# Second layer of batches 4 to 7 of a Nyström attention and MLP kernel: eight half-size block products replaced by seven

## The chip, the cores and the metric

The kernel runs on one core of one Trainium2 chip. The metric is the device time of one execution in microseconds, the median of several runs.

## The reference

The reference is an attention of the Nyström kind followed by an MLP with a residual. q, k and v are 8 batches x 8 heads x 576 tokens x 64. The attention's output, with heads side by side, is x: 8 batches x 576 tokens x 512 columns.

```python
xn = (x - mu) / np.sqrt(var + 1e-06) * g_ln
ch = np.maximum(xn @ w_ch1, 0.0) @ w_ch2
return (x + ch)
```

w_ch1 is 512 x 2048 (the first layer) and w_ch2 is 2048 x 512 (the second layer). The document is about the product with w_ch2.

## The kernel before, in words

The matmul operands are fp16, and sums are fp32 in PSUM. Tokens lie in 36 blocks of 128 rows; two batches are nine blocks. An even batch has four blocks in its second layer and leaves its last 64 tokens to the next batch; an odd batch has five.

For each batch the work is attention (`attention2`, for batches 1, 2, (3, 4), (5, 6), 7 together as grouped), rows of x (`rows_of`), statistics of x (`measure`, `deviations`), first layer (`first_layer`) and second layer (`second_layer`). The first layer writes the hidden values, after the ReLU, transposed into `hT`: 128 partitions x 16 chunks of the hidden dimension x tokens, fp16. One `hT` tile exists for even and one for odd batches. ScalarE or VectorE empties the first layer's PSUM tiles (`chunk`), whichever is estimated to be free first.

`second_layer(b)` takes block after block. For each it holds one of four PSUM banks, adds up 16 matmuls (one per chunk of the hidden dimension, hT as the stationary operand of 128x128, `w2_16` as the moving one of 512 columns), and then `finish_block` lets VectorE multiply by the token's 1/deviation and add x, into `xblk`. `store` writes the block out by two DMAs on SyncE's queue (SP). The very last block is done in two halves of 256 columns.

W2 comes in through the ring of six staging buffers ("stg") that also takes q, k and v. Its tiles of 4608 bytes per partition are free again when their cast to fp16 is done.

**What sets the order.** All instructions of all engines keep the order in which the program emits them. While it builds the program, the class `Clock` (line 72) keeps an estimate of when each engine is free and each tile written; `took` (line 108) holds an engine's cost per operation and `note` (line 122) books an instruction. `run` (line 1340) has four generators (attentions, first layers, rows of batch 0, second layers), each of which yields the estimated time at which its next step could start. It takes the first of them, in this order, that could start now. So the second layer is the filling where nothing else can go. Between two steps `help_out` (line 1268) hands out side work: stores, loads, casts on GpSimd, and on VectorE transposes, sums and statistics, wherever the estimate says that the engine is about to be free. `first_layer(b)` may start once `second_layer(b - 1)` has begun. Attention holds one of the four banks while it iterates (`mine`), and the first layer's `product_of_heads` (line 1103) needs two free banks.

`keep_tail` (line 1185) is a GpSimd copy at the begin of an even batch's second layer, which puts its last 64 tokens into the next batch's `hT`.

Of the kernel before, what the change touches and what calls it, by code (L numbers as in the profile page):

```python
# [20 lines left out]
def kernel(  # L21
# [40 lines left out]
    def name_of(x):  # L62
        return x.tensor.name if hasattr(x, "tensor") else x.name

    parted = {}

    def key_of(ap):

        n = name_of(ap)
        return f"{n}:{ap.offset // parted[n]}" if n in parted else n  # L70

    class Clock:


        WAY = 55.0

        def __init__(self):
            self.free = dict.fromkeys(("PE", "DVE", "Activation", "Pool", "SP"), 0.0)
# [13 lines left out]

        def calm(self, n):

            return self.fetched if self.count + n >= self.mark else 0.0

        def at(self, *tiles):
            return max([self.wrote.get(name_of(t), (0.0, ""))[0] for t in tiles] + [0.0]) + self.WAY

        def at_key(self, ap):  # L100
            return self.wrote.get(key_of(ap), (0.0, ""))[0] + self.WAY

        def idle(self, *tiles):

# [3 lines left out]
        def took(self, i, e, n, m):  # L108
            op = type(i).__name__
            if e == "Activation":  # L110
                return 190 + 0.79 * n
            if e == "Pool":
                return 100 + 0.92 * n if "Copy" in op else 280 + 1.76 * n
            if "Stats" in op:
                return 690 if m > 100 else 180
            if n == 1024:
                return 900
            if "Transpose" in op:
                return 110 + 1.15 * n
            return 140 + 1.15 * max(n, m if "Reduce" in op else 0)  # L120

        def note(self, i):
            e = str(i.engine).rsplit(".", 1)[-1]
            outs = [a.bass_ap for a in i.outs if hasattr(a, "bass_ap")]
            ins = [a.bass_ap for a in i.ins if hasattr(a, "bass_ap")]
            size = [[k for _, k in a.ap] for a in outs + ins]
            count = []
            for dims in size:
                n = 1
                for k in dims[1:]:  # L130
                    n *= k
                count.append(n)
            ready = 0.0
            for a in ins:
                t, who = self.wrote.get(key_of(a), (0.0, e))
                if who != e:
                    ready = max(ready, t + self.WAY)
            for a in outs:
                for t, who in (self.wrote.get(key_of(a), (0.0, e)), self.used.get(key_of(a), (0.0, e)),
                               (self.begun.get(key_of(a), 0.0), "")):  # L140
                    if who != e:
                        ready = max(ready, t + self.WAY)
            if type(i).__name__ == "InstDMACopy":
                start = max(self.free[e], ready)
                self.free[e] = start + (580 if e == "SP" else 100)
                self.wire = max(start + 1650, self.wire) + count[0] * size[0][0] * 4 / 370.0
                done = self.wire + 600
                start = done
            elif e == "PE":
                cols = count[0]  # L150
                self.count += 1
                if self.count >= self.mark:
                    self.mark += self.BLOCK
                    ready = max(ready, self.fetched)
                    self.fetched = max(self.now(), ready) + self.FETCH
                rows_, cols_ = tuple(i.tile_size)
                self.cells.append((self.now(), cols / 2.4 * rows_ * cols_ / 128 ** 2))
                if tuple(i.tile_size) == (128, 128):
                    if self.small:
                        self.free[e] = max(list(self.lanes.values()) + [self.free[e]]) + 100  # L160
                        self.small, self.lanes = False, {}
                    start = max(self.free[e], ready)
                    self.free[e] = start + max(cols / 2.4 + 3, 56)
                    done = self.free[e] + 160
                else:
                    if not self.small:
                        self.small, self.lanes = True, {}
                        self.free[e] += 100
                    lane = tuple(i.tile_position)
                    start = max(self.free[e], ready, self.lanes.get(lane, 0.0))  # L170
                    self.lanes[lane] = start + max(cols / 2.4, 70)
                    self.free[e] = start + 6
                    done = self.lanes[lane] + 160
            else:
                start = max(self.free[e], ready)
                done = self.free[e] = start + self.took(i, e, count[0], max(count[1:] + [0]))
            for a in ins:
                n = key_of(a)
                self.used[n] = max(self.used.get(n, (0.0, e)), (done, e))
            for a in outs:  # L180
                n = key_of(a)
                self.wrote[n] = max(self.wrote.get(n, (0.0, e)), (done, e))

    clock = Clock()

# [1029 lines left out]
    def blocks_0_and_1():  # L1215
# [10 lines left out]
        for u in range(2):  # L1226
            finish_block(0, u, accs[u][0])
            banks.release(accs[u][1])

    def second_layer(b):  # L1230
        hT = hTs[b]
        if b == 0:
            yield from blocks_0_and_1()
        blocks = range(4 + b % 2) if b else (2, 3)
        for u in blocks:
# [32 lines left out]
    def help_out(hurry=False):  # L1268

        while True:  # L1270
            now = clock.now() + 100
            begun = len(unstored)
            while unstored and (hurry or clock.at(unstored[0][1]) <= now):
                store(*unstored.pop(0))
            for c in sets:
                if c.loads:
                    if (stage.next("stg") <= now and clock.free["SP"] <= now + 500
                            and clock.wire <= now + AHEAD):
                        c.next_load()
                        begun = -1  # L1280
                    break
            for c in sets:
                if c.casts:
                    if clock.free["Pool"] <= now + 600 and c.cast_ready() <= now + 600:
                        c.next_cast()
                        begun = -1
                    break
            if clock.free["DVE"] <= now + lead():
# [23 lines left out]
    current, begun_first = [0], [0]  # L1312

    def attentions():
        for c in sets:
# [5 lines left out]
    def first_layers():  # L1321
        for b in range(B):
            yield lambda: 0.0 if b == 0 or (b in ready and current[0] == b - 1
                                            and (b <= LAST_WHOLE or len(centered) == 4)) else NEVER
            yield from first_layer(b)
            first_done.add(b)
            if b == 0:
                keep_tail(0)

# [108 lines left out]
```

## Time and profile before

| | us |
|---|---|
| median of three runs (290.29 to 291.4) | 291.2 |
| the profiled execution | 291.77 |
| its span, first to last instruction | 290.0 |
| TensorE matmuls busy | 274.0 (94%) |
| VectorE busy | 187.1 (65%) |
| ScalarE busy | 160.1 (55%) |
| GpSimd busy | 141.7 (49%) |

The mean granted clock of TensorE is 0.987 of full speed. A matmul of 128x512 in the second layer lasts 385 ns on average in the records, since neighbours overlap; the pace of a stream of them is read from what waits for them. The profile names engines PE (TensorE), PEld (its weight loads), DVE (VectorE), ACT (ScalarE), POOL (GpSimd) and SP (SyncE). Most lines of the code are reached through two helpers, so nearly all matmuls carry line 240 and nearly all other instructions line 234; the names of the tiles tell them apart. In a window's row the columns are length, busy us and count for PE, PEld, DVE, ACT and POOL, then granted clock, the DMA engines' share and GB/s. In a timeline row they are start, length, engine, line, operation, shapes, count, and in brackets the engine's idle time before and what ended it.

The last load of q, k and v ends near 150 us. From then on only stores use the queue.

### The profile page before, as it was taken

The numbers are of one execution on the slowest core, as the hardware profiler recorded it, in microseconds if no ns is written. First come the engines' busy times: TensorE is split into PE (matmuls) and PEld (weight loads), VectorE is DVE, ScalarE is ACT, GpSimd is POOL, SyncE is SP. The second block draws the span as 40 slices with busy tenths as digits, with TensorE's granted clock in tenths as the row PEclk, the third lists the DMA queues.
The fourth block names the chain that finished last, engine by engine and source line by source line (L and its number), as shares of the span: only waits on it lengthen the run. The fifth ranks groups of instructions, "written<-read, shape, count | busy, mean of one in ns | idle before, by whom it ended". The sixth has DMA issues, their size and how long they took to land.

```text
span 290.0 us, 8202 instructions
## 1 busy us (share of the span) xinstructions
PE 274.0 (94%) x3426; PEld 147.9 (51%) x3426; DVE 187.1 (65%) x412; ACT 160.1 (55%) x282; POOL 141.7 (49%) x171
## 2 busy tenths in 40 slices
PE   7888996998899999999889999999999999999994
PEld 7644553345444565444445645556445644564443
DVE  3558975699999875997888284878265373422222
ACT  2567955128851787448889755567277732570000
POOL 4378779899998999999980008400003001000000
PEclk9999999599999999999999999999999999999999
DMA  7999999979545499873800112111120113112333
GB/s 244 381 390 386 387 388 390 299 243 329 168 161 150 133 307 335 240 242 108 287 8 3 36 31 48 39 38 36 41 64 12 37 36 75 37 38 61 80 76 75
DMA packets 23374, 46.68 MB, mean 161 GB/s; under 512 B 2212, under 2 KB 2472, under 8 KB 23336
## 3 DMA queue, kind: packets, MB, share of 16 engines
q1 hardware_dynamic: 23176, 46.02, 49.5%
q8 instruction: 27, 0.44, 0.6%
q10 hardware_dynamic: 160, 0.13, 0.2%
q14 instruction: 11, 0.09, 0.1%
HBM read 36.70 MB, written 9.44 MB: 159 GB/s over the span
## 4 chain that ended last, share of the span: by engine, by line
PE 53%; DVE 14%; POOL 13%; DMA 12%; issue 4%; ACT 1%; SPq 1%; POOLq 0%; DVEq 0%; ACTq 0%
PE bank L240 38%; PE psh L240 12%; DMA stg<-in_v_dram 5%; DMA wstg<-in_moe_w_ch_dram 5%; POOL nat L234 4%; POOL asum L234 3%; POOL natv L234 3%; DVE m L234 2%; DVE six L234 2%; DVE w L234 2%; DMA stg<-in_k_dram 2%; DVE part L234 2%; DVE xblk L234 1%; DVE xT L234 1%; POOL w L234 1%
## 5 line engine op out<-in xcount | busy, mean ns | idle before, releaser
L240 PE MATMUL bank<-w,hT 128*128 128x512 f16 (+1 forms) x592 | 148.5, 379 | 0.5 <-issue 0.5
L240 PEld LDWEIGHTS <-hT 128*128 128x128 f16 x592 | 54.8, 98 | 53.6 <-issue 9.9
L234 ACT ACTIVATE hT<-psh 128x576 f16<-128x576 f32 x111 | 69.0, 651 | 22.3 <-PE psh L240 21.6
L240 PE MATMUL psh<-ea,m 128*128 128x288 f16 x512 | 76.5, 286 | 3.1 <-ACT hT L234 1.8
L240 PEld LDWEIGHTS <-m 128*128 128x128 f16 x512 | 48.6, 98 | 27.6 <-issue 9.4
L234 DVE SCALAR_TENSOR_TENSOR xblk<-bank,rstd,xblk 128x512 f32<-128x512 f32 (+1 forms) x37 | 26.8, 728 | 34.8 <-PE bank L240 34.8
L234 POOL CAST natv<-stg 64x1152 f16<-64x1152 f32 (+1 forms) x23 | 26.7, 1161 | 31.4 <-PE pscv L240 22.4
L234 POOL CAST nat<-stg 128x1152 f16<-128x1152 f32 x28 | 32.5, 1180 | 2.0 <-DMA stg<-in_k_dram 1.1
L234 POOL TENSOR_TENSOR ea<-ea,lns 128x576 f16<-128x576 f16 x14 | 17.8, 1286 | 31.6 <-ACT lns L234 31.6
L234 ACT COPY xblk<-bank 128x512 f32<-128x512 f32 (+1 forms) x34 | 19.0, 595 | 18.5 <-PE bank L240 18.4
L234 DVE BATCH_NORM_STATS2 six<-xblk 128x6 f32<-128x512 f32 x36 | 24.3, 676 | 2.6 <-ACT xblk L234 2.5
L234 DVE STREAM_TRANSPOSE xT<-nat 128x576 uint32<-128x576 uint32 x28 | 21.5, 766 | 2.5 <-POOL nat L234 2.5
L234 ACT CAST m<-bank 128x512 f16<-128x512 f32 x30 | 17.0, 588 | 7.0 <-PE bank L240 7.0
L234 DVE CAST m<-bank 128x512 f16<-128x512 f32 x18 | 12.4, 687 | 12.9 <-PE bank L240 12.8
L234 DVE TENSOR_REDUCE part<-xT 128x32 f16<-128x576 f16 x28 | 20.4, 746 | 0.3
L234 ACT ACTIVATE lns<-psd 128x576 f32<-128x576 f32 x16 | 10.3, 646 | 18.1 <-PE psd L240 15.1
L234 POOL TENSOR_TENSOR asum<-asum 128x256 f32<-128x256 f32 (+1 forms) x28 | 17.2, 615 | 2.2
L234 POOL COPY hT<-hT 128x1024 f16<-128x1024 f16 x4 | 4.2, 1038 | 28.9 <-PE bank L240 28.9
L234 POOL TENSOR_TENSOR asum<-nat 128x512 f32<-128x512 f16 x14 | 16.8, 1202 | 1.1
L234 DVE SCALAR_TENSOR_TENSOR st<-st,bank 128x128 f16<-128x128 f16 (+2 forms) x36 | 11.1, 308 | 7.3 <-PE bank L240 7.3
L240 PE MATMUL bank<-zcbd,ea 128*128 128x256 f16 (+1 forms) x80 | 14.5, 275 | 1.2 <-DVE m L234 0.8
L234 DVE TENSOR_SCALAR hT<-psh 128x576 f16<-128x576 f32 x17 | 12.8, 753 | 4.1 <-PE psh L240 3.6
(114 smaller groups left out, 277.6 us busy)
## 6 DMA issues: line engine op xcount, KB each, us to landing
stg<-in_q_dram SPq DMA_DIRECT2D x16, 576.0 KB, 5.5
stg<-in_k_dram SPq DMA_DIRECT2D x16, 576.0 KB, 5.2
stg<-in_v_dram SPq DMA_DIRECT2D x16, 576.0 KB, 6.2
out_dram<-xblk SPq DMA_DIRECT2D x70, 128.0 KB, 2.3
wstg<-in_moe_w_ch_dram SPq DMA_DIRECT2D x16, 512.0 KB, 7.0
out_dram<-xblk ACTq DMA_DIRECT2D x2, 64.0 KB, 2.1
out_dram<-xblk SPq DMA_DIRECT2D x2, 64.0 KB, 2.2
g_rows<-in_moe_g_ln_dram SPq DMA_DIRECT2D x1, 2.0 KB
```

Source lines behind the costliest of these rows:

```text
L234: return lambda *args, **kw: keep(getattr(self.engine, op)(*args, **kw))
L240: keep(nc.tensor.matmul(o, l, r, start=start, stop=stop, tile_position=(rb, cb), skip_group_check=(skip or cb != 0)))
```

## The change

For batches 4 to 7 the four blocks of 128 tokens that the second layer has in common are computed as one product of 512 tokens x 2048 x 512 columns, cut in halves along all three dimensions. Instead of eight products of halves there are seven (256 tokens x 1024 x 256 columns each, 16 matmuls of 256 columns), of mixed operands. The fifth block of batches 5 and 7 stays as it was.

- *Mixes of W2*, once: four tiles t1 to t4 of 128 x 8 x 256 fp16 by GpSimd, each in four subtractions of 512 elements per partition (`mix_w2`). They use four of the six staging buffers, after the last load; two more buffers become s1 and s2, the scratch tiles for mixes of hT.
- *Mixes of hT*, per batch: s1 = h21 + h22, s2 = s1 - h11, h21 = h11 - h21 in place (`mix_ahead`, once the batch's first layer is emitted and s1 and s2 are free), and h12 = h12 - s2 in place within the products. Each is two VectorE instructions of 1024 elements per partition.
- *Products*, per batch, in the order P1 to P7: h11 w11 into bank a; h12 w21 into bank e; s2 t2 on top of a; s1 t1 into bank c; h21 t3 on top of a; h12 w22 on top of c; h22 t4 on top of a. After a product VectorE adds its bank to a quarter of x, two instructions of 128x256, 14 per batch in place of four of 128x512. A product on top of a bank can begin when the bank has been added. s1 and s2 are set free for the next batch after P4.
- *The builder's estimates*: other costs per operation for GpSimd and VectorE, an overlap of neighbouring instructions on one engine, another transfer rate and a delay that grows with the queue, other costs of small matmuls, and dependencies tracked by parts of a tile. They add no instruction but decide about the order of all of them.

Cut to its core:

```diff
 class Clock:
+        OVERLAP = {"Activation": 110, "DVE": 80, "Pool": 30}
...
-            return self.fetched if self.count + n >= self.mark else 0.0
+            return self.fetched if self.count + n + (20 if late() else 0) >= self.mark else 0.0
...
             if e == "Pool":
+                if n == 1024 and name_of(i.outs[0].bass_ap) in mixed_:
+                    return 2080
+                if "Ptr" in op:
+                    return 100 + 1.29 * n
                 return 100 + 0.92 * n if "Copy" in op else 280 + 1.76 * n
+            if n == 1152 and "Copy" in op:
+                return 760
...
+            if n >= 512 and (n == 576 or op == 'InstTensorCopy'):
+                return 100 + 1.13 * n
             if n == 1024:
-                return 900
+                return 690 if name_of(i.outs[0].bass_ap) in mixed_ else 900
...
-                self.wire = max(start + 1650, self.wire) + count[0] * size[0][0] * 4 / 370.0
-                done = self.wire + 600
+                self.wire = max(start + 1650, self.wire) + count[0] * size[0][0] * 4 / 385.0
+                done = self.wire + 600 + min(2200, 0.6 * (self.wire - start - 1650))
...
-                    self.lanes[lane] = start + max(cols / 2.4, 70)
-                    self.free[e] = start + 6
+                    self.lanes.update((x, start + max(cols / 2.4, 30)) for x in lane)
+                    self.free[e] = start + (8 if rows_ == 64 and cols < 128 else 4)
...
-                done = self.free[e] = start + self.took(i, e, count[0], max(count[1:] + [0]))
+                done = start + self.took(i, e, count[0], max(count[1:] + [0]))
+                self.free[e] = done - self.OVERLAP[e]
...
+    def mix_w2():
...
+            if n <= 4:
+                x, y = ((w12, w11), (w22, w2_mix[0]), (w22, w12), (w21, w2_mix[min(1, n - 1)]))[n - 1]
+                for k in range(0, HK, 2):
+                    w2_left.append((t[:, k:k + 2, :], x[:, k:k + 2, :], y[:, k:k + 2, :]))
+        if w2_left:
+            o, x, y = w2_left.pop(0)
+            pool.tensor_tensor(out=o, in0=x, in1=y, op=ALU.subtract)
+
+    def mix(o, left, right, op, k):
+        n = ds(k, 4)
+        dve.tensor_tensor(out=o[:, n, :], in0=left[:, n, :], in1=right[:, n, :], op=op)
...
+    def seven_products(b):
+
+        while b not in h_mixed:
+            yield lambda: NEVER if b not in h_mixed and len(w2_mix) < 6 else 0.0
+            if b not in h_mixed:
+                if hTs[b].name not in mixed_:
+                    yield lambda: clock.at_key(hTs[b][:, MCH - 1, 0:P])
+                mix_ahead()
...
+        def product(to, left, right, first=True):
+            bank, t = to
+            for i in range(2):
+                for k in range(HK):
+                    yield ((lambda: 0.0) if i or k % 4 else
+                           lambda: max(clock.at_key(left[:, k, 0:P]), clock.at_key(right[:, k, :]),
+                                       0.0 if k else clock.idle(banks.tiles[bank])))
+                    MM(t[:, i, :], left[:, k, ts(i, P)], right[:, k, :],
+                       start=first and k == 0 and i == 0, stop=k == HK - 1, skip=True)
+
+        def add(half, col, to, done=False):
+            for i in range(2):
...
+                dve.scalar_tensor_tensor(out=o, in0=to[1][:, i, :], scalar=rstds[b][:, u:u + 1],
+                                         in1=o, op0=ALU.mult, op1=ALU.add)
...
+        yield banks.next
+        a = bank()
+        yield from product(a, h11, w11)
+        early = b in rstds
+        if early:
+            add(0, 0, a)
+        yield banks.next
+        e = bank()
+        yield from product(e, h12, w21)
+        yield from finished(b)
+        if not early:
+            add(0, 0, a)
+        yield from product(a, s2, t2, False)
+        add(0, 0, e)
+        banks.release(e[0])
+        yield banks.next
+        c = bank()
+        add(0, 1, a)
+        for k in (0, 4):
+            mix(h12, h12, s2, ALU.subtract, k)
+        yield from product(c, s1, t1)
+        in_use.clear()
+        add(1, 1, c)
+        yield from product(a, h21, t3, False)
+        add(1, 1, a)
+        yield from product(c, h12, w22, False)
+        add(0, 1, c, True)
+        banks.release(c[0])
+        yield from product(a, h22, t4, False)
+        add(1, 0, a, True)
+        banks.release(a[0])
+
     def second_layer(b):
...
         blocks = range(4 + b % 2) if b else (2, 3)
+        if b >= FAST:
+            yield from seven_products(b)
+            blocks = blocks[4:]
```

`FAST` is 4. In `help_out`, after the casts and before VectorE's other side work, `mix_w2` is called where no load is left and GpSimd is about to be free, and `mix_ahead` where the six tiles exist and VectorE is about to be free.

More of the change, by code (lines that the diff above doesn't have):

```diff
@@ L63, in name_of, with keys_of @@
         return x.tensor.name if hasattr(x, "tensor") else x.name
-    parted = {}
+    parted, mixed_ = {}, set()
     def key_of(ap):
+        return keys_of(ap)[0]
+    def keys_of(ap):
         n = name_of(ap)
-        return f"{n}:{ap.offset // parted[n]}" if n in parted else n
+        if n not in parted:
+            return [n]
+        at = [ap.offset]
+        for step, k in list(ap.ap)[1:]:
+            if step >= parted[n]:
+                at = [o + step * i for o in at for i in range(k)]
+        if n in mixed_:
+            return [f"{n}:{o // parted[n]}:{int(o % parted[n] >= 256)}" for o in at]
+        return [f"{n}:{o // parted[n]}" for o in at]
     class Clock:
         WAY = 55.0
+        OVERLAP = {"Activation": 110, "DVE": 80, "Pool": 30}
         def __init__(self):
@@ L101, in at_key, with idle_key @@
             return self.wrote.get(key_of(ap), (0.0, ""))[0] + self.WAY
+        def idle_key(self, ap):
+            n = key_of(ap)
+            return max(self.wrote.get(n, (0.0, ''))[0], self.used.get(n, (0.0, ''))[0]) + self.WAY
         def idle(self, *tiles):
@@ L132, in note @@
                 count.append(n)
+            reads = [n for a in ins for n in keys_of(a)]
+            writes = [n for a in outs for n in keys_of(a)]
             ready = 0.0
[L134 to L140, printed above, removed]
+            for n in reads:
+                t, who = self.wrote.get(n, (0.0, e))
+                if who != e or e != "PE":
+                    ready = max(ready, t + (self.WAY if who != e else 0.0))
+            for n in writes:
+                for t, who in (self.wrote.get(n, (0.0, e)), self.used.get(n, (0.0, e)),
+                               (self.begun.get(n, 0.0), "")):
                     if who != e:
@@ L154, in note @@
                     ready = max(ready, self.fetched)
-                    self.fetched = max(self.now(), ready) + self.FETCH
+                    self.fetched = max(self.now(), ready) + (self.FETCH if self.wire > self.now() else 3000)
                 rows_, cols_ = tuple(i.tile_size)
@@ L167, in note, with late @@
                         self.small, self.lanes = True, {}
[L168 to L173 removed]
+                        self.free[e] += 95
+                    lane = [(a, c) for a in range(i.tile_position[0], i.tile_position[0] + rows_, 32)
+                            for c in range(i.tile_position[1], i.tile_position[1] + cols_, 32)]
+                    start = max([self.free[e], ready] + [self.lanes.get(x, 0.0) for x in lane])
+                    self.lanes.update((x, start + max(cols / 2.4, 30)) for x in lane)
+                    self.free[e] = start + (8 if rows_ == 64 and cols < 128 else 4)
+                    done = self.lanes[lane[0]] + 160
             else:
                 start = max(self.free[e], ready)
[L176 to L178 removed]
+                done = start + self.took(i, e, count[0], max(count[1:] + [0]))
+                self.free[e] = done - self.OVERLAP[e]
+            for n in reads:
                 self.used[n] = max(self.used.get(n, (0.0, e)), (done, e))
[L180 to L181 removed]
+            for n in writes:
                 self.wrote[n] = max(self.wrote.get(n, (0.0, e)), (done, e))
+    current = [0]
+    def late():
+        return current[0] >= 3
     clock = Clock()
@@ L1228, in blocks_0_and_1 @@
             banks.release(accs[u][1])
+    HK, HN, FAST = MCH // 2, DM // 2, 4
+    w2_mix, w2_left, h_left, h_mixed, in_use = [], [], [], set(), []
+    w11, w12 = w2_16[:, 0:HK, 0:HN], w2_16[:, 0:HK, HN:DM]
+    w21, w22 = w2_16[:, HK:MCH, 0:HN], w2_16[:, HK:MCH, HN:DM]
+    def mix_w2():
+        if not w2_left:
+            t = stage.tile([P, HK, HN], FP16, name="w2mix", tag="stg")
+            parted[t.name] = HN
+            w2_mix.append(t)
+            n = len(w2_mix)
+            if n <= 4:
[5 more added lines that the diff above has]
+            pool.tensor_tensor(out=o, in0=x, in1=y, op=ALU.subtract)
@@ new lines, in mix, with parts_of, mix_ahead @@
+    def mix(o, left, right, op, k):
+        n = ds(k, 4)
+        dve.tensor_tensor(out=o[:, n, :], in0=left[:, n, :], in1=right[:, n, :], op=op)
+    def parts_of(b):
+        hT = hTs[b]
+        return (hT[:, 0:HK, 0:256], hT[:, HK:MCH, 0:256], hT[:, 0:HK, 256:512],
+                hT[:, HK:MCH, 256:512])
+    def mix_ahead():
+        b, i, k = h_left.pop(0)
+        h11, h12, h21, h22 = parts_of(b)
+        s1, s2 = w2_mix[4][:], w2_mix[5][:]
+        if i == k == 0:
+            assert not in_use
+            in_use.append(b)
+        if i == 0:
+            n = hTs[b].name
+            mixed_.update((name_of(s1), name_of(s2), n))
+            for seen in (clock.wrote, clock.used):
+                seen.update({f"{n}:{m}:{h}": seen[f"{n}:{m}"] for m in range(MCH) for h in range(2)
+                             if f"{n}:{m}" in seen})
+            mix(s1, h21, h22, ALU.add, k)
+        elif i == 1:
+            mix(s2, s1, h11, ALU.subtract, k)
+        else:
+            mix(h21, h11, h21, ALU.subtract, k)
+        if not any(x[0] == b for x in h_left):
+            h_mixed.add(b)
@@ new lines, in seven_products, with bank @@
+    def seven_products(b):
[5 more added lines that the diff above has]
+                mix_ahead()
+        t1, t2, t3, t4, s1, s2 = [t[:] for t in w2_mix]
+        h11, h12, h21, h22 = parts_of(b)
+        j0 = 9 * (b // 2) + 4 * (b % 2)
+        def product(to, left, right, first=True):
[9 more added lines that the diff above has]
+            for i in range(2):
+                u = 2 * half + i
+                x = x_blk[j0 + u]
+                o = x[:, ts(col, HN)]
+                dve.scalar_tensor_tensor(out=o, in0=to[1][:, i, :], scalar=rstds[b][:, u:u + 1],
+                                         in1=o, op0=ALU.mult, op1=ALU.add)
+                if done:
+                    unstored.append((j0 + u, x, ts(0, DM), False))
+                    x_blk.pop(j0 + u)
+        def bank():
+            t = banks.hold([P, 2, HN])
+            return banks.last, t
+        yield banks.next
[29 more added lines that the diff above has]
+        banks.release(a[0])
@@ L1234, in second_layer @@
         blocks = range(4 + b % 2) if b else (2, 3)
+        if b >= FAST:
+            yield from seven_products(b)
+            blocks = blocks[4:]
+            if not blocks:
+                hTs.pop(b)
         for u in blocks:
@@ L1287, in help_out @@
                     break
+            if (begun >= 0 and (w2_left or len(w2_mix) < 6) and not any(c.loads for c in sets)
+                    and clock.free["Pool"] <= now + 100 and (w2_left or stage.next("stg") <= now)):
+                mix_w2()
+                begun = -1
+            if (begun >= 0 and h_left and len(w2_mix) == 6 and clock.free["DVE"] <= now + 100
+                    and (h_left[0][1:] != (0, 0)
+                         or not in_use and max(clock.at_key(hTs[h_left[0][0]][:, MCH - 1, 0:P]),
+                                *[clock.idle_key(t[:, k, :]) for t in w2_mix[4:]
+                                  for k in (3, HK - 1)]) <= now)):
+                mix_ahead()
+                begun = -1
             if clock.free["DVE"] <= now + lead():
@@ L1310, in help_out @@
                 return
-    current, begun_first = [0], [0]
+    begun_first = [0]
     def attentions():
@@ L1326, in first_layers @@
             first_done.add(b)
+            if b >= FAST:
+                h_left.extend((b, i, k) for i in range(3) for k in (0, 4))
             if b == 0:
```

## The prediction

> **What bounds the kernel now.** I read the page first, then the busy time by stage, then single instructions. The page has TensorE (PE) busy through almost the whole span and VectorE (DVE) half idle in the last third. The last row is the clock that TensorE was granted.
>
> ```profile
> span 290.0 us, 8202 instructions
> ...
> PE   7888996998899999999889999999999999999994
> PEld 7644553345444565444445645556445644564443
> DVE  3558975699999875997888284878265373422222
> ACT  2567955128851787448889755567277732570000
> POOL 4378779899998999999980008400003001000000
> PEclk9999999599999999999999999999999999999999
> ```
>
> The edited work, the second layer of batches 4 to 7, begins with a GpSimd copy at 187.3 us and runs to the end. A table of windows cut where the first layers of batches 5, 6 and 7 begin and end gives, after each window and its length, busy us and instructions of PE, weight loads, DVE, ACT and GpSimd:
>
> ```profile
> 203.40:210.90 7.50, 7.50 (x64) 3.31 (x67) 1.50 (x2) 1.71 (x3) 0.00 (x0) 1.00 0.25 58
> 210.90:218.00 7.10, 7.00 (x209) 3.39 (x189) 4.87 (x17) 5.15 (x11) 0.44 (x1) 1.00 0.22 53
> 218.00:230.60 12.60, 12.60 (x118) 7.80 (x119) 5.78 (x10) 10.02 (x18) 2.12 (x2) 1.00 0.03 7
> 230.60:245.40 14.80, 14.80 (x89) 6.77 (x87) 7.14 (x16) 3.97 (x8) 0.00 (x0) 1.00 0.30 68
> 245.40:260.00 14.60, 14.60 (x121) 8.82 (x121) 6.26 (x9) 9.46 (x16) 1.04 (x1) 1.00 0.16 36
> 260.00:286.30 26.30, 26.21 (x138) 13.19 (x135) 5.79 (x9) 1.08 (x4) 0.00 (x0) 1.00 0.29 66
> ```
>
> TensorE waits for next to nothing from 190 us on; a cycle saved there is a cycle off the end, unless a new wait eats it. A busy TensorE need not be at its peak, so I take the pace from what VectorE finishes in the last stage, where TensorE does nothing else. Each line is the finishing step of one block of 128 tokens (start, length):
>
> ```profile
> 265.49 0.75 DVE L234 SCALAR_TENSOR_TENSOR xblk<-bank,rstd,xblk 128x512 f32<-128x512 f32 x1 [2.70 <-PE bank L240]
> ...
> 279.30 0.75 DVE L234 SCALAR_TENSOR_TENSOR xblk<-bank,rstd,xblk 128x512 f32<-128x512 f32 x1 [2.70 <-PE bank L240]
> 282.76 0.75 DVE L234 SCALAR_TENSOR_TENSOR xblk<-bank,rstd,xblk 128x512 f32<-128x512 f32 x1 [2.70 <-PE bank L240]
> 284.50 0.48 DVE L234 SCALAR_TENSOR_TENSOR xblk<-bank,rstd,xblk 128x256 f32<-128x256 f32 x1 [1.00 <-PE bank L240]
> 286.25 0.48 DVE L234 SCALAR_TENSOR_TENSOR xblk<-bank,rstd,xblk 128x256 f32<-128x256 f32 x1 [1.26 <-PE bank L240]
> ```
>
> From 265.49 to 279.30 lie four blocks of 16 matmuls of 512 columns: 13.81/64 = 0.2158 us each. From 282.76 to 286.25 lie two half blocks of 16 matmuls of 256 columns: 3.49/32 = 0.1091 us each. That second pace is exactly the shape that the change multiplies.
>
> **TensorE: what is removed and added.** Per batch 64 matmuls of 512 columns go (64 x 0.2158 = 13.81 us) and 7 x 16 = 112 of 256 columns come (112 x 0.1091 = 12.22 us). Saved: 1.59 us a batch, 6.36 us in four, all in a stage without slack. The fifth block of batches 5 and 7 stays.
>
> A rule speaks against this. The Trainium skill, "TensorE: Matmul & The Clock Gate", Part 3 (The mechanism), says that a weight load overlaps running matmuls only where its row group differs. A load of hT takes 98 ns here (592 of them, mean). Laid end to end a product's matmul would be 0.098 + 0.109 = 0.207 us and a batch 23.2 us: 9.4 us lost, four times over. But the two half blocks above, with all four row groups in every load, show 0.109 us with a load each, so the load was hidden. I take the row. The margin is thin (98 under 109), and only 32 such matmuls in a row are on show, not 112.
>
> **VectorE: adds.** Per batch 4 finishing steps of 0.75 us go and 14 of 128x256 come, at 0.48 us (the last two lines): 6.7 - 3.0 = +3.7 us. Most lie beside the next product, in the other bank.
>
> **VectorE: mixes.** Per batch 8 subtractions or sums of 1024 fp16 elements. The nearest row is the centring of W1, also two fp16 operands of 1024; the tile view gives min/median/max:
>
> ```profile
> L234 DVE TENSOR_TENSOR w<-w,less x8: 830/927/1625, 74.7 to 84.3; 128x1024 f16<-128x1024 f16 x8
> ```
>
> These eight ran where GpSimd was over 90% busy. The Trainium skill, "VectorE: DVE Perf Modes", The perf-mode tier table, gives tensor_tensor on two-byte SBUF operands two elements a cycle; its estimate from the same page (about 150 cycles fixed, 0.96 GHz) is 0.69 us for 1024, and 1.22 us at one a cycle. The row's minimum of 0.83 us lies under the one-a-cycle price, so the fast mode was on, and from 190 us on GpSimd was busy for only 3.6 of 96.3 us. I take 0.69 and keep 0.93 and 1.22 as the far end: 5.5 us a batch, up to 9.8.
>
> Together VectorE needs 6.7 + 5.5 = 12.2 us for a batch's products, as much as TensorE. Over the stage it had 41.7 busy of 96.3 us; 15 for adds and, for the 26 mixes that fall inside it (batch 4's first six come before), 18 make 75 of 90. It fits on average; the question is where it bunches up. Behind a mix in VectorE's order stand the adds, and behind an add stands the next product that accumulates in that bank.
>
> Where other streams run (first layers of 5, 6, 7; attention of 7) TensorE has something else to do and I charge 0.3 us in all. The tight seam is batch 6 to 7, after 260 us: one pair of scratch tiles exists, so batch 7's first six mixes start only after batch 6's fourth product. Counting from that product's start, TensorE reaches batch 7's third product at 6 x 1.745 = 10.5 us. VectorE's queue until then, from 0.2 us on: twelve adds 5.8, eight mixes 5.5, and some 0.3 for handing over, so 11.8 us, or 10.6 if each of the twenty overlaps its neighbour by 0.06 (two zcbd products of 0.41 us end to end took 0.75). That is 0.1 to 1.3 us of waiting. In batch 7 itself the sixth product waits for two mixes and an add behind each other: 0.2 to 0.4 us. I charge 0.9 us for the tail.
>
> **GpSimd: W2's mixes.** 16 subtractions of 512 fp16 elements. Nearest rows: 128x512 sums of asum, 1.20 us, and ea's 576-element products, 1.29 us: 19.2 us. GpSimd finishes its last loads' sums at 151.5 us and next works at:
>
> ```profile
> 173.83 3.60 POOL L234 CAST natv<-stg 128x1152 f16<-128x1152 f32 x3 [22.36 <-PE pscv L240]
> ```
>
> So 19.2 us fit into 22.4 us. Behind them on its queue stand those casts of v and four normalisations; late by one mix they would slip 1.2 us, and TensorE needs them only with batch 7's attention at 215 and batch 5's rows near 185. Cost taken: nothing. Without that gap, up to 19 us would lie ahead of batch 4's second layer. The last two of the six scratch tiles come from v's staging at 177.4 us, ten microseconds before batch 4 needs them.
>
> **Stores.** Their number is the same, but four finish at once after the sixth and four after the seventh product. Issuing one took SP 0.51 us (median): four are 2.0 us, under the fifth block's 3.5. Cost nothing, at most 0.3.
>
> **The builder's corrected estimates** reorder everything, also before 187 us, with no operation added. There is one place to gain:
>
> ```profile
> 48.00:50.00 2.00, 0.51 (x21) 0.15 (x7) 0.66 (x1) 1.33 (x2) 2.00 (x3) 1.00 1.05 387
> 50.00:52.00 2.00, 0.84 (x10) 0.41 (x11) 1.97 (x5) 0.00 (x0) 1.91 (x3) 0.56 1.05 381
> 52.00:54.00 2.00, 2.00 (x6) 0.69 (x5) 1.80 (x6) 0.00 (x0) 1.84 (x3) 0.50 1.01 350
> 54.00:56.00 2.00, 2.00 (x14) 0.63 (x13) 0.70 (x2) 0.91 (x2) 1.73 (x3) 0.50 0.96 257
> 56.00:58.00 2.00, 2.00 (x22) 0.56 (x20) 0.96 (x3) 0.43 (x1) 1.49 (x2) 0.73 0.89 246
> ```
>
> TensorE stood still for 2.65 us behind a VectorE job queued on a late GpSimd cast, and then had about half its clock until 57 us (2.9 us more): 5.6 us. Better estimates may remove it, or make another such hole. Bounds -5.6 and +5.6; with no row to decide, I take 0.
>
> **The sum.** 291.77 (profiled execution; span 290.0) - 6.36 + 0.9 + 0.3 = 286.6; the runs' median of 291.2 lies 0.6 under that execution, so 286.0.
>
> **Rivals.**
> - *The hole at 48 us closes as well*: 286.0 - 5.6 = 280.4. For it: the transfer, GpSimd and VectorE estimates that led to it are the ones changed. Against: GpSimd's estimates for W1's scaling become shorter, transfers faster but later to land; which wins isn't in the trace. 0.22.
> - *Another hole opens*: 286.0 + 5.6 = 291.6. 0.10.
> - *Two held banks starve the others*: attention of batch 7 holds one of four banks from 210.7 to 220.3 us, two products hold two, and a first layer's product of heads needs two. Batch 6's first layer slips up to 6 us. Its cover is batch 5's second layer (12.2 + 3.5 us), of which it needs some 4, so this is mostly hidden; half uncovered, 289. 0.10.
> - *VectorE becomes the bound, and the kernel is slower*: if a mix costs 1.22 us, the tail's queue grows by 8 x 0.53 = 4.2 us, the sixth product of batch 7 by 1.1, and two seams between batches 4 to 6 by about 1 each: 7.4 on top of 1.2 charged, against 6.36 saved: 286.0 + 7.4 = 293.4. It cancels the gain from about 1.15 us a mix. Against it: the 0.83 us minimum. 0.14.
> - The likeliest case, 286.0 (284.3 to 287.7 by the tail's ends and the stores): 0.44.
>
> A doubt over the whole, that the change does not take effect, is small: the branch is taken for every batch from 4 on.
>
> **How the numbers follow.** Within 0.5% (289.7 to 292.7) is about what a measurement can't tell from no change. Faster: 0.44 + 0.22 + 0.08 of the banks = 0.74. Same: 0.09 of the second hole, 0.03 of VectorE, 0.02 of the banks = 0.14. Slower: 0.11 of VectorE and 0.01 = 0.12. The range 280 to 291.7 leaves out VectorE's case (0.14) and the outer part of the first rival (0.06).
>
> **What would show it.** Right: 448 matmuls of 256 columns for batches 4 to 7 with 0.109 us between them where TensorE is alone; mixes near 0.69 us; W2's mixes between 151 and 174 us; the last pure stage, 26.3 us now, down to about 24. Wrong: mixes over 0.9 us, TensorE waiting for xblk or hT mixes after 260 us by more than 2 us, a clock row under 9 in a new slice, or a first layer 6 that starts after the attention's bank is free and then runs without filler.

## The result, and the profile after

The changed kernel takes 287.02 us (median; 286.43 to 287.35), the kernel before 290.98 beside it: a ratio of 0.9864, with a 95% interval of 0.9838 to 0.9890. The forecast was 286.0, a microsecond less. The profiled execution took 287.15 us, its span 285.4.

The page of the kernel after, the rows that answer to those of before:

```profile
span 285.4 us, 8685 instructions
...
DVE  3558985999999754998798842899697299747761
...
PEclk9999999999999999999999999999999999999999
```

VectorE is far busier in the last third, where it was half idle, and the dip in the granted clock, in the eighth slice of before, is gone. From 257.44 us on TensorE again does nothing but second layers. Its timeline (start, length, instruction, count):

```profile
260.17 1.91 PE L272 MATMUL bank<-w2mix,hT 128*128 128x256 f16 x16
261.92 1.91 PE L272 MATMUL bank<-w,hT 128*128 128x256 f16 x16
263.67 1.91 PE L272 MATMUL bank<-w2mix,hT 128*128 128x256 f16 x16
265.41 3.66 PE L272 MATMUL bank<-w,hT 128*128 128x256 f16 x32
268.90 3.66 PE L272 MATMUL bank<-w2mix 128*128 128x256 f16 x32
272.40 1.91 PE L272 MATMUL bank<-w2mix,hT 128*128 128x256 f16 x16
```

The lengths overlap, the starts are what counts: product follows product at 1.74 or 1.75 us, 0.109 us a matmul, through batch 6's last three products and all seven of batch 7 (its last two follow from 274.14 and 275.89 us). The third product of batch 7 (first half of the row at 268.90) waits for nothing. VectorE in the same stretch, part of it:

```profile
258.63 0.88 DVE L266 SCALAR_TENSOR_TENSOR xblk<-bank,rstd,xblk 128x256 f32<-128x256 f32 x2 [2.37 <-PE bank L272]
259.42 1.28 DVE L266 TENSOR_TENSOR hT<-hT,w2mix 128x1024 f16<-128x1024 f16 x2
...
267.42 0.88 DVE L266 SCALAR_TENSOR_TENSOR xblk<-bank,rstd,xblk 128x256 f32<-128x256 f32 x2
269.11 0.87 DVE L266 SCALAR_TENSOR_TENSOR xblk<-bank,rstd,xblk 128x256 f32<-128x256 f32 x2 [0.81 <-PE bank L272]
```

From 258.63 to 268.3 us it has no pause: its last work for the third product ends 0.6 us before that product starts. Two adds take 0.87 us and two mixes 1.28, less than twice 0.48 and 0.68, since neighbours overlap by 0.08 us. W2's mixes lie where they were expected, in GpSimd's gap, at 1.12 us each end to end:

```profile
151.94 4.50 POOL L266 TENSOR_TENSOR w2mix<-w 128x512 f16<-128x512 f16 x4
...
165.29 4.50 POOL L266 TENSOR_TENSOR w2mix<-w,w2mix 128x512 f16<-128x512 f16 x4
172.66 1.16 POOL L266 CAST natv<-stg 128x1152 f16<-128x1152 f32 x1 [2.87 <-PE pscv L272]
```

**Where the time came from.** I cut both executions at the GpSimd copy that opens batch 4's second layer, before first and after second:

```profile
187.33 1.04 POOL L234 COPY hT<-hT 128x1024 f16<-128x1024 f16 x1 [3.83 <-PE bank L240]
187.99 1.13 POOL L266 COPY hT<-hT 128x1024 f16<-128x1024 f16 x1 [4.35 <-issue]
```

The rest takes 102.6 us before and 97.4 after. So all of the 4.6 us between the spans, and a little more, comes from the late stage. The first 188 us, in which the order changed and the mixes of W2 and the first of hT came in, gave nothing, though the pause at 48.5 us and its half clock had gone. A second execution of after (`again_after` below) has its cut at 186.7 us and again 97.4 us behind it: the late stage repeats, while the early part differs by 1.3 us between two executions of one kernel. The windows of after where the pause was:

```profile
48.00:50.00 2.00, 2.00 (x59) 0.95 (x46) 1.05 (x6) 1.12 (x2) 1.71 (x2) 1.00 1.08 395
50.00:52.00 2.00, 2.00 (x18) 0.92 (x17) 2.00 (x5) 1.44 (x3) 1.70 (x2) 1.00 1.01 366
```

Batch 1's first layer begins at 57.3 us instead of 63.6, batch 2's at 91.7 instead of 94.6, batch 3's at 134.9 instead of 134.6: the lead is lost between 60 and 135 us. TensorE's longest waits from 60 to 150 us in after (what was waited for, then us in total, times, longest; "issue" is a wait for which the profile shows no cause):

```profile
PE bank L272 <- DVE st L266: 1.5, 2, 1.1
PE bank L272 <- issue: 1.4, 1, 1.4
PE bank L272 <- DVE part L266: 1.3, 1, 1.3
```

All of TensorE's pauses between 62 and 150 us come to 4.6 us before and 8.2 after, which is about half of the lead that was lost. The rest stays open. One candidate is GpSimd as the limit of this stretch: it is busy for 82.5 of 88 us before and 82.2 after, and the last of its sums ends at 151.5 us before and 152.0 after. But in the runs below that end does not go with the time: it lies at 152.9 us in the faster `back_dma` and at 149.8 in the slower `back_pe`.

### The profile page after: what moved, and what is told of

It reads as the page before. It is cut to its first block, busy times and chain, and to the rows that moved or that the text cites. A ratio compares the mean times of both kernels' runs of the same rounds, so it can differ in the third digit from the quotient of the medians.

```text
span 285.4 us, 8685 instructions
## 1 busy us (share of the span) xinstructions
PE 267.0 (94%) x3620; PEld 165.5 (58%) x3620; DVE 216.0 (76%) x480; ACT 162.5 (57%) x286; POOL 159.2 (56%) x187
## 4 chain that ended last, share of the span: by engine, by line
PE 47%; POOL 18%; DVE 14%; DMA 13%; issue 4%; ACT 1%; SPq 1%; POOLq 0%; DVEq 0%; ACTq 0%
PE bank L272 31%; PE psh L272 13%; POOL natv L266 6%; DMA stg<-in_v_dram 6%; DMA wstg<-in_moe_w_ch_dram 5%; POOL asum L266 4%; POOL nat L266 4%; DVE w L266 3%; DVE xblk L266 2%; DVE xT L266 2%; DMA stg<-in_k_dram 2%; POOL ea L266 2%; DVE part L266 1%; DVE m L266 1%; DVE six L266 1%
## 5 line engine op out<-in xcount | busy, mean ns | idle before, releaser
L272 PE MATMUL bank<-w,hT 128*128 128x512 f16 (+1 forms) x528 | 108.7, 335 | 1.4 <-issue 1.4
L266 ACT ACTIVATE hT<-psh 128x576 f16<-128x576 f32 x114 | 71.3, 651 | 18.5 <-PE psh L272 16.6
L272 PE MATMUL psh<-ea,m 128*128 128x288 f16 x512 | 77.4, 286 | 3.1 <-ACT hT L266 1.3
L272 PEld LDWEIGHTS <-hT 128*128 128x128 f16 x656 | 60.6, 98 | 32.7 <-issue 7.1
L272 PEld LDWEIGHTS <-m 128*128 128x128 f16 x512 | 47.9, 97 | 24.8 <-issue 10.0
L266 DVE SCALAR_TENSOR_TENSOR xblk<-bank,rstd,xblk 128x256 f32<-128x256 f32 (+1 forms) x77 | 39.2, 541 | 24.6 <-PE bank L272 24.5
L266 ACT COPY xblk<-bank 128x512 f32<-128x512 f32 (+1 forms) x32 | 17.8, 589 | 11.9 <-PE bank L272 11.8
L272 PE MATMUL bank<-w2mix,hT 128*128 128x256 f16 x128 | 16.5, 273 | 0.0
L272 PE MATMUL bank<-w2mix 128*128 128x256 f16 x128 | 16.0, 273 | 0.0
L272 PE MATMUL bank<-w,zt 64*32 64x512 f16 x256 | 14.2, 386 | 0.5 <-ACT less L266 0.4
```

The lines of the kernel that those rows point to most:

```text
L266: return lambda *args, **kw: keep(getattr(self.engine, op)(*args, **kw))
L272: keep(nc.tensor.matmul(o, l, r, start=start, stop=stop, tile_position=(rb, cb), skip_group_check=(skip or cb != 0)))
```

## Experiments

The planner, in what follows, is the part of the program that decides about the order: the class `Clock` with its estimates, and `run`. My theory was that the change is two changes that act apart: seven products that take some 5 us off the late stage, and an order of instructions that gives back early what it wins. The first rival was that the closed pause at 48 us made the whole gain. Four kernels ran beside one another; before took 291.52 us there.

**The estimates alone** (`est_only`).

```diff
-    HK, HN, FAST = MCH // 2, DM // 2, 4
+    HK, HN, FAST = MCH // 2, DM // 2, 8
...
-            if (begun >= 0 and (w2_left or len(w2_mix) < 6) and not any(c.loads for c in sets)
+            if (FAST < B and begun >= 0 and (w2_left or len(w2_mix) < 6) and not any(c.loads for c in sets)
```

> The corrected estimates alone: the seven products are switched off (batch limit 8), so the second layer is as before. My theory, that the two halves of the change act apart and the estimates give back as much as they win: the half-clock patch at 50 to 57 us is gone, pauses between 60 and 150 us take its place, batch 4's second layer begins near 188.0 us instead of 187.3, and the time is 291.7 us (290.5 to 293). The rival, that the closed pause is what made the kernel faster and the products give nothing: 286 to 287 us.

Measured: 293.06 us, ratio 1.0048 (1.0019 to 1.0078): by the ratio 1.4 us slower than before, and just over the range I gave. The rival's 286 to 287 is excluded. Of its trace, an execution of 296.08 us, I read only where TensorE stands: there is no pause over 0.6 us between 40 and 70 us and no half clock there, and pauses of 1.2, 1.4 and 2.8 us end at 75.7, 98.8 and 129.1 us, the places at which after has its own.

**The products alone** (`prod_only`): the constants of before are put back.

```diff
-        OVERLAP = {"Activation": 110, "DVE": 80, "Pool": 30}
+        OVERLAP = {"Activation": 0, "DVE": 0, "Pool": 0}
...
-                if "Ptr" in op:
-                    return 100 + 1.29 * n
...
-                self.wire = max(start + 1650, self.wire) + count[0] * size[0][0] * 4 / 385.0
-                done = self.wire + 600 + min(2200, 0.6 * (self.wire - start - 1650))
+                self.wire = max(start + 1650, self.wire) + count[0] * size[0][0] * 4 / 370.0
+                done = self.wire + 600
...
-                    self.lanes.update((x, start + max(cols / 2.4, 30)) for x in lane)
-                    self.free[e] = start + (8 if rows_ == 64 and cols < 128 else 4)
+                    self.lanes[lane] = start + max(cols / 2.4, 70)
+                    self.free[e] = start + 6
```

> The seven products alone: costs, overlap, transfer and TensorE constants of the planner are those of before; only the tracking of tile parts that the products need stays. My theory: the pause at 48.5 us and the half clock until 57 us are there as before, batch 4's second layer begins at 187.3 us, and from there to the end it takes 97.4 us instead of 102.7: 285.7 us (285 to 286.5). The rival that the products give nothing: 291 us.

Measured: 287.19 us, ratio 0.9831 (0.9797 to 0.9866): faster by 4.9 us by the ratio, by 4.3 by the medians. I had expected 285.7 of 290.98, a ratio of 0.982; in us it lies 0.7 over my range. The early part is that of before, pause and half clock included, as the windows of this kernel show (the third column from the end is the clock):

```profile
48.00:50.00 2.00, 0.78 (x42) 0.42 (x40) 0.39 (x1) 1.18 (x3) 2.00 (x3) 1.00 1.04 389
50.00:52.00 2.00, 0.58 (x10) 0.33 (x11) 1.97 (x5) 0.18 (x1) 1.91 (x3) 1.00 1.05 388
52.00:54.00 2.00, 2.00 (x8) 0.70 (x6) 1.93 (x7) 0.00 (x0) 1.84 (x3) 0.70 1.02 369
54.00:56.00 2.00, 2.00 (x13) 0.56 (x12) 1.11 (x3) 1.33 (x2) 1.92 (x3) 0.50 0.92 279
```

Its late stage takes 98.6 us, 1.2 more than after's; what shows there are 1.7 us of pauses between 231 and 236 us, in which attention's small matmuls wait for VectorE. VectorE was late because one mix took 1.58 us instead of 0.68 while GpSimd worked on `ea` beside it:

```profile
232.61 3.13 POOL L259 TENSOR_TENSOR ea<-ea,lns 128x576 f16<-128x576 f16 x2 [44.50 <-PE bank L265]
233.03 1.58 DVE L259 TENSOR_TENSOR w2mix<-w2mix,hT 128x1024 f16<-128x1024 f16 x1
```

No mix in after took over 0.70 us, and only 0.2 us of pause shows in its late stage before the last matmul. So in after's order no mix is held up like this, and what its estimates cost lies before the late stage. That GpSimd is the cause was not tested by a run of its own. The product of the two ratios, 1.0048 x 0.9831 = 0.988, agrees with after's 0.9864: the parts add within the intervals, each about a microsecond either way. An interaction smaller than that would not show.

**Each mix twice** (`mix_twice`).

```diff
         dve.tensor_tensor(out=o[:, n, :], in0=left[:, n, :], in1=right[:, n, :], op=op)
+        dve.tensor_tensor(out=o[:, n, :], in0=o[:, n, :], in1=o[:, n, :], op=ALU.max)
```

> After, with each VectorE mix of hT followed by a second instruction of the same size on the same tile (the larger of it and itself, so no value changes): 8 x 0.64 = 5.1 us more VectorE work per batch. My theory, that VectorE has hardly any slack at the seam of batch 6 to 7 (its instructions stand end to end from 258.6 to 268.3 us, 0.6 us before the third product needs them): that product waits some 4.5 us, the sixth of batch 7 some 0.9, the seams before 1 to 2 in all, so 293.5 us (291.5 to 295.5). The rival, that VectorE at 76% busy hides it: below 288.5 us.

Measured: 298.34 us, ratio 1.0217 (1.0175 to 1.0259); 11 us above after's 287 and 2.8 over my range. TensorE in the tail, batch 7's third product first:

```profile
268.97 3.66 PE L272 MATMUL bank<-w,hT 128*128 128x256 f16 x32
276.92 5.32 PE L272 MATMUL bank<-w2mix 128*128 128x256 f16 x32 [4.29 <-DVE xblk L266]
282.08 1.91 PE L272 MATMUL bank<-w2mix,hT 128*128 128x256 f16 x16
284.72 1.91 PE L272 MATMUL bank<-w,hT 128*128 128x256 f16 x16 [0.73 <-DVE xblk L266]
```

The waits, 4.29 and 0.73 us, are those expected (4.5 and 0.9). The row after the first wait takes 5.32 us instead of 3.66: in this execution the clock was half from 277.1 to 280.5 us. Of the seams before, two products waited 0.91 and 0.90 us for VectorE (from 206.6 and 232.1 us), as I gave them. What I had not counted is attention of batch 7, whose matmuls waited 1.73 us for VectorE from 238.5 us, behind a mix and its double of 1.58 and 1.65 us, again beside GpSimd's work on `ea`. So VectorE has no slack at the seam, and a mix of twice the length makes the kernel slower than before.

**No mixes** (`mixes_out`).

```diff
-        n = ds(k, 4)
-        dve.tensor_tensor(out=o[:, n, :], in0=left[:, n, :], in1=right[:, n, :], op=op)
+        return
...
-        t1, t2, t3, t4, s1, s2 = [t[:] for t in w2_mix]
+        t1, t2, t3, t4 = [t[:] for t in w2_mix[:4]]
         h11, h12, h21, h22 = parts_of(b)
+        s1, s2 = h22, h12
```

> After, with the mixes of hT left out: the products take unmixed halves of hT, so the output is not the reference's; W2's mixes, the matmuls and the adds stay. My theory, that no product waits for a mix: no more than 0.5 us faster than after, 286.5 to 287.1 us. The rival, that what lacks to the 6.36 us of saved TensorE time is waiting for mixes: 285.9 us.

Measured: 288.59 us, ratio 0.9874 (0.9835 to 0.9914), no faster than after (0.9864), and 1.5 us over the range I gave. The planner does not book the mixes here, so the order may change too; the trace tells the two apart. The late stage, where all but the first mixes of hT lie, takes 97.7 us without them and 97.4 in after. What is longer lies before it: a pause of 2.0 us that ends at 127.9 us, without a cause in the profile (1.4 in after), and 3.4 us of half clock from 128.6 us. As they stand, the mixes cost nothing; the rival is not supported.

**One group of estimates put back at a time.** The second question was what in the planner closes the pause at 48 us and what opens the later ones. In each kernel the named group of after's constants is replaced by that of before, as in the diff of `prod_only`; the products stay. Before took 291.36 us beside them.

> After, with the transfer estimate of before (370 GB/s, no delay that grows with the queue). If the later landings of the new estimate closed the pause at 48.5 us, it and the half clock to 57 us are back, and the time is 2 to 6 us above after, a ratio to before of 0.995 to 1.005. If the transfers' estimate is what costs the pauses at 75, 98 and 126 us, those are gone instead and the ratio is 0.975 to 0.981. Neither: 0.986.

> After, without the overlap of neighbouring instructions (110, 80 and 30 ns) and the wait on the own engine's results. If VectorE is now thought to be free too early, so that TensorE is sent to wait for it at 75, 98 and 126 us (1.1, 1.3 and 1.4 us in after), those shrink and the ratio to before is 0.977 to 0.982. If not, 0.986.

> After, with the costs of before for GpSimd's scaling of W1 (1181 ns in place of 760), VectorE's casts of 1152 and its operations of 576. If these closed the pause at 48.5 us, it is back with the half clock: a ratio to before of 0.995 to 1.005. If they open the later pauses: 0.977 to 0.982. Neither: 0.986.

> After, with TensorE's estimates of before (70 ns for a small matmul in place of 30, one lane per tile position, a fixed time to fetch instructions). If the planner now believes small matmuls to be over too soon and sends TensorE into the pauses at 75, 98 and 126 us, those shrink: a ratio to before of 0.977 to 0.982. If these constants closed the pause at 48.5 us, 0.995 to 1.005. Neither: 0.986.

| put back | us | ratio to before | 95% interval |
|---|---|---|---|
| transfers (`back_dma`) | 285.19 | 0.9790 | 0.9758 to 0.9823 |
| overlap (`back_overlap`) | 287.12 | 0.9877 | 0.9839 to 0.9915 |
| costs (`back_took`) | 287.44 | 0.9880 | 0.9850 to 0.9910 |
| TensorE (`back_pe`) | 290.76 | 0.9979 | 0.9948 to 1.0010 |

None of the four brings the pause of 2.65 us at 48 us back, and none brings half clock there: between 40 and 62 us TensorE pauses for 0.0, 0.4, 0.3 and 0.7 us. So none of the groups alone closed it. With the transfers of before the kernel is faster, and the pauses at 98 and 126 us are gone, while that at 74 us grows from 1.1 to 1.4 and new ones of 0.9 and 1.1 us lie at 77 and 182 us. The pause at 126 us has no cause in the profile and differs between two executions of after, 1.4 and 0.8 us, so it isn't the planner's alone. Without the TensorE constants of after the kernel is slower: the pause at 96 us is longer (1.7 instead of 1.3 us), one of 1.0 us lies at 65, and that at 126 is gone. Its late stage takes 99.7 us, 2.2 more than after's; a mix takes 1.58 us at 235.6 us beside GpSimd's `ea`, and attention waits 0.8 us behind it, as in `prod_only`. That is against what I thought of these constants.

**Once more, on one chip** (five rounds, before 291.49 us): after as it is, the faster version, half of its edit, and two groups at once.

```diff
-                done = self.wire + 600 + min(2200, 0.6 * (self.wire - start - 1650))
+                done = self.wire + 600
```

The diff is that of `no_delay`; `again_back_dma` has 370 for 385 as well, and `back_dma_took` also the costs.

> After, unchanged, measured beside the next three on one chip: a ratio to before of 0.984 to 0.989, and no half clock or one of 3.4 us.

> After with the transfer estimate of before, once more, in five rounds beside after. If the 0.979 of its first measurement is the kernel's and not the chip's: 0.976 to 0.982, below after by at least 1.5 us. If it was chance: as after.

> After with the new rate of 385 GB/s but without the delay that grows with the queue: landings are believed earliest of all. If the delay is what makes the planner late with loads and casts (the cause of what the transfer estimate costs): 0.975 to 0.983. If the rate is: as after, 0.984 to 0.989.

> After with two groups of estimates of before, the transfers' and the operations' costs. If the groups' effects add (transfers -0.7%, costs +0.2%): a ratio of 0.978 to 0.984. If the order of the instructions reacts to the sum and not to the parts, it lies outside, on either side; then no single constant carries the blame.

| kernel | us | ratio to before | 95% interval |
|---|---|---|---|
| after (`again_after`) | 287.10 | 0.9859 | 0.9829 to 0.9889 |
| transfers of before (`again_back_dma`) | 285.24 | 0.9805 | 0.9776 to 0.9835 |
| without the delay (`no_delay`) | 285.78 | 0.9829 | 0.9797 to 0.9861 |
| transfers and costs (`back_dma_took`) | 286.10 | 0.9822 | 0.9794 to 0.9849 |

After repeats. The version with the old transfer estimate is 1.9 us faster than after by the medians here, and was by about as much the first time; the two intervals in this table just overlap. It is the fastest kernel of this study. Whether the delay or the rate is its cause stays open: `no_delay` lies between, at the edge of what I gave for the delay. The sum of two groups came out as the sum of their parts within the intervals.

## Why the prediction was right, step by step

- **TensorE, 6.36 us saved.** Held. The pace of 0.109 us with a weight load per matmul, read from 32 matmuls of before, holds over 160 in one stream, and the loads stay hidden (98 ns; busy 15.6 of 17.4 us between 260.2 and 277.6). The rule of the Trainium skill, "TensorE: Matmul & The Clock Gate", Part 3 (The mechanism), that a load overlaps only where its row group differs, does not hold here; by it the kernel would have lost. The same section also lets a load run ahead into a background buffer, which the prediction left out and which fits the 0.109 us; that it is the cause, no run here shows.
- **The late stage, 6.36 - 1.2 = 5.2.** Measured 102.6 - 97.4 = 5.2. The sum is right and its parts are not: the tail, charged with 0.9, has no wait at all. What was lost instead is the end (from the last add's end to the last store 3.6 us, before 3.3, as I had allowed), some 0.3 us in three more changes from large to small matmuls at 0.09 us each (24 in place of 21), and, for the rest of some 0.6 us, irregular gaps that I did not trace further.
- **VectorE.** A mix took 0.68 us against 0.69 taken, an add 0.48. Twenty instructions at the seam fit because neighbours overlap by 0.08 us, more than the 0.06 that I gave as the better end. The far end of my range was the dangerous one indeed: `mix_twice`, at about 1.3 us a mix, gives 298, while I had 293.4 for 1.22. The working of the waits was right: 4.3 and 0.7 us in the tail (4.2 and 1.1 in the prediction) and 1.8 at two seams before (2). Two terms were not in the sum, attention's own wait for VectorE (1.7 us) and the half clock behind the longest wait (1.7). The far end itself was too near for single mixes: beside GpSimd's work they took 1.58 us in three kernels, though none did in after.
- **GpSimd.** 151.9 to 169.8 us, hidden, as worked out (17.9 us instead of 19.2).
- **Two held banks.** Batch 6's first layer began at 211.7 us and ran before attention held its bank; nothing of it is seen in after.
- **The estimates, taken as nothing, -5.6 to +5.6.** Alone they cost 1.4 us. The likeliest case and the first rival were not the alternatives I made of them: the hole did close, and the likeliest time came true all the same, since other pauses opened. That this term came out near nothing was luck; I had no row for it. The step that was wrong is that time won at 48 us reaches the end. Where the hole lay the price of 5.6 us was about right, since batch 1's first layer begins 6.3 us earlier in after; by batch 3's first layer nothing of it is left. What the half clock alone costs can't be read from the runs of before. Beside the first four experiments the five whose mean clock was 0.986 to 0.988 took 291.65 us (median) and the two at 0.999 and 1.000 took 290.35 and 290.54, 1.2 us less. But beside the last four kernels two at 0.988 took 290.00 and 290.42 (a third 294.90), and the two at 1.000 took 289.96 and 290.66, no less.

Why one constant opens a pause and another closes it is not settled: of the planner only results were measured, and each change of it moves the order everywhere.

## What to carry to other kernels

Read the pace of a shape that a change will multiply from a place where the kernel before already runs it alone; here 32 matmuls at the very end fixed the largest term to within what could be measured. Where a change trades one engine's work for another's, add up the second engine's queue between two waits, not its share of the span: VectorE was busy for 76% and had 0.6 us to spare. And measure a planner's constants apart from the work they came with: here the new transfer estimate cost 0.5 to 0.7% and the new TensorE costs gained 1.2%, and only putting them back one at a time showed it. A pause that closes early in a kernel is not yet time won: here 6 us of lead at 57 us were gone at 135 us.

## What was not expected of the hardware

Half clock followed pauses of TensorE under three microseconds, but not always, and not always for the same length: 6.8 us of it with the pause of 2.65 us in the profiled execution of before, 3.4 us with 2.64 us in `prod_only`, 3.4 us after two pauses of 1.0 us at 87.4 and 88.7 us in `back_overlap`, and none after 1.4 us in after, nor after 2.1 us at 126.6 us in `back_overlap`. `back_dma` and `again_back_dma` are one and the same kernel, with the same pause of 1.1 us at 182 us: 3.4 us of half clock from 184.6 us in the first, none in the second. So such a patch belongs to an execution and not only to a kernel, and the length of the pause alone does not decide it. Between the first matmul and the last, every patch in these traces is 3.4 or 6.8 us long.

What a patch costs seems to depend on where it lies. In the tail of `mix_twice`, where the end waits for TensorE alone, 3.4 us of half clock made a row of 32 matmuls 1.66 us longer. In `back_pe` the profiled execution had 6.8 us of it from 23.3 us on and took 290.76 us; the execution of that kernel at full clock took 290.77.

A mix of hT by VectorE, 0.68 us as a rule, took 1.58 us where a GpSimd instruction on `ea` ran at the same time (`prod_only`, `mix_twice`, `back_pe`). In `back_pe` GpSimd's instruction began at 235.35 us and ended at 236.63, and the mix that began at 235.60 ended at 237.18: 0.55 us after GpSimd was done, as if it had done its work only then.
